# When a second MoE's weight splits begin and when its token lists are read: one planner change

## The chip, the cores and the metric

The kernel runs on one core of one Trainium2 chip. The metric is device time in microseconds, the median of repeated executions. A profiled execution, taken once, gives the trace. The engines are named as in the profile: PE (TensorE matmul), PEld (its weight loads), DVE (VectorE), ACT (ScalarE), POOL (GpSimd) and SP (SyncE, which here only issues transfers and reads values out of memory into registers).

## The reference, cut to what matters

```python
x = attention(q, k, v)             # 4 x 576 tokens, 8 heads of 64, causal window of 128
g = softplus(x @ w_in)             # first MoE: 2304 tokens, 512 -> 2048
x = g @ w_out                      #            2048 -> 512
logits = x @ w_gate                # second MoE: 8 experts, top 2
noisy = logits + softplus(x @ w_noise) * noise
top2_w = softmax of the two largest of noisy
for e in range(8):                 # for the tokens that chose expert e
    out[mask] += top2_w * (relu(x[mask] @ w1[e]) @ w2[e])    # 512 -> 1024 -> 512
```

Everything is float32. The kernel keeps precision by splitting a float32 operand into a high and a low part and adding three products (high times high, low times high, high times low).

## The kernel before, in words

**First MoE.** The 2304 tokens are nine chunks of 256. The hidden width of 2048 is cut into 16 slices, and one slice of one chunk is a step: there are 144 steps (`NT`), each of twelve `h` matmuls (512 to 128) and, three steps later, six `y` matmuls (128 to 512). Two PSUM buffers hold `h`, so the `h` of a step can start only when DVE's `sl` (the last operation that reads `h`) of two steps before is done. When a chunk is through, its gate logits, top 2 and ranks are computed (`lg`, the `r_...` rows, `mcum`), and POOL scatters a record of each token and choice into four copies of a table `rect` in memory.

**Second MoE.** Tokens are worked on in groups, each of one expert. Groups 0 to 3 are "early" pairs (256 tokens each), which are counted out as soon as the first six chunks are routed. Then come 14 late "pairs" mixed with five "singles" (128 tokens) and two optional singles. A pair's weights are eight tiles of 512 KB, and its work is eight items, each of twelve `h` matmuls and six `z` or `y` matmuls. For a group the kernel

1. reads the expert and the start of its list from a small table (SP, a value load; tables `c_Eearlyeo`, `c_Lpairseo`, `c_Lsingleseo`, which DVE works out in one-row operations, line 870),
2. reads its list out of the four copies of `rect` (SP, four `rk<-rect` transfers, `g_rows`, line 1031),
3. merges the four (DVE, two `rc<-rk` reductions, lines 1035 and 1036),
4. gathers the tokens (POOL, `xg<-x1buf,rc`, line 1046),
5. transposes them (PE, `t<-ident,xg`, line 201) and splits them into `xh` (ACT) and `xl` (DVE),
6. adds the scaled results into `out` (POOL, `out<-ys,rc`, line 1251).

**Weights.** Line 1110 loads a tile, into one of four extra buffers (`raw2`, shown as `raw`) or into the 24-slot ring that the first MoE's weights also live in (`rawp`). A split makes `whi` of it (ACT, line 1139) and `wlo` (DVE, line 1137). At most five tiles stand split at a time (`NSPLIT`).

**What sets the order.** Each engine runs its instructions in the order in which they were emitted. That order is decided at build time by a planner (`Order`). Work is entered as chains of steps, `chain((engine, cost, function, key, needs), ...)`, with modelled costs in microseconds. A heap pops the step whose modelled time has come, and `after=` puts a chain's first step that much later. `("tab", 0)` marks the early table as given out, `("tab", 1)` the late one. `pump()` issues weight loads as far as buffers and tables allow, and asks for splits as far as the ring has room. The wait of an instruction for its data is added after that and holds up everything behind it on its engine.

Of the kernel before, what the change touches and what calls it, by code (L numbers as in the profile page):

```python
# [25 lines left out]
class Order:  # L26
# [11 lines left out]
    def chain(self, *steps, after=0.0):  # L38

        heapq.heappush(self.heap, (self.now + after, self.count, steps, 0))  # L40
        self.count += 1
# [71 lines left out]
def moe_chain_kernel(ctx, tc, qk, v, w_in, w_out, w_gate, w_noise, noise, w1, w2, out):  # L113
    nc = tc.nc
    PE, ACT, DVE, POOL, SP = nc.tensor, nc.scalar, nc.vector, nc.gpsimd, nc.sync
# [820 lines left out]
    def early_table(c):  # L936
        tb, cnt = counted(c, "E")
        per = tb.above("per", cnt, TB["jfull"], NJ // 2, OP.is_ge)
        inc = tb.upto("inc", per)
        ex, r = tb.first_of(TB["qe"], "q", NEARLY, inc, per)  # L940
        tb.finish("early", ex, r, None, NEARLY)
        a, b = tb.row("a", [E]), tb.row("b", [E])
        tb.tensor_sub(b, inc, per)
        tb.tensor_scalar(a, inc, float(NEARLY), None, op0=OP.min)
        tb.tensor_scalar(b, b, float(NEARLY), None, op0=OP.min)
        tb.tensor_sub(a, a, b)
        off = TB["off"] = tb.row("off", [E])
        tb.tensor_scalar(off, a, 2.0 * P, None, op0=OP.mult)
        chain(*tb.steps, (None, 0.0, early_lists, ("tab", 0), (("scat", c),)))

    def late_table(c):
        tb, cnt = counted(c, "L")
        off, e8, qp, qs_ = TB["off"], TB["e8"], TB["qp"], TB["qs"]
        tb.tensor_sub(cnt, cnt, off)
        me = tb.above("me", cnt, TB["jm"], NJ, OP.is_gt)
        per = tb.above("per", cnt, TB["jpair"], NJ // 2, OP.is_gt)
        se = tb.row("se", [E])
        tb.scalar_tensor_tensor(se, per, -2.0, me, op0=OP.mult, op1=OP.add)
        pinc = tb.upto("pinc", per)
        sinc = tb.upto("sinc", se)  # L960
        ptot, stot = pinc[:, E - 1:E], sinc[:, E - 1:E]


        ex, r = tb.first_of(qp, "A", NLATE, pinc, per, off)
        lastr = tb.row("lastr", [E])
        tb.scalar_tensor_tensor(lastr, per, 2.0 * P, off, op0=OP.mult, op1=OP.add)
        all8 = tb.row("all8", [1])
        tb.tensor_scalar(all8, stot, float(E), None, op0=OP.is_equal)
        ok = tb.row("ok", [NLATE])
        eq = tb.row("eq", [NLATE])  # L970
        tb.tensor_tensor(eq, qp, ptot.to_broadcast([1, NLATE]), OP.is_equal)
        tb.tensor_tensor(eq, eq, all8.to_broadcast([1, NLATE]), OP.mult)
        tb.tensor_tensor(ok, qp, ptot.to_broadcast([1, NLATE]), OP.is_lt)
        tb.tensor_add(ok, ok, eq)
        tb.finish("pairs", ex, r, ok, NLATE)


        gq = tb.row("gq", [NSING])
        tb.tensor_sub(gq, qs_, stot.to_broadcast([1, NSING]))
        half = tb.row("half", [NSING])  # L980
        tb.tensor_scalar(half, gq, 0.0, None, op0=OP.mult)
        for j in range(1, NSING, 2):
            tb.scalar_tensor_tensor(half, gq, float(j), half, op0=OP.is_equal, op1=OP.add)
        gp = tb.row("gp", [NSING])
        tb.tensor_sub(gp, gq, half)
        tb.tensor_scalar(gp, gp, 0.5, float(NLATE), op0=OP.mult, op1=OP.add)
        exb, rb_ = tb.first_of(gp, "B", NSING, pinc, per, off)
        tb.scalar_tensor_tensor(rb_, half, float(P), rb_, op0=OP.mult, op1=OP.add)
        okb = tb.row("okb", [NSING])
        tb.tensor_tensor(okb, gp, ptot.to_broadcast([1, NSING]), OP.is_lt)  # L990
        cm = tb.row("cm", [NSING, E7])
        tb.tensor_tensor(cm, jb(sinc[:, :E7], NSING, E7), ib(qs_, NSING, E7), OP.is_le)
        exs = tb.total("exs", cm, NSING)
        rs = tb.of_expert("rs", exs, lastr, NSING)
        own = tb.row("own", [NSING])
        tb.tensor_tensor(own, qs_, stot.to_broadcast([1, NSING]), OP.is_lt)
        for x, y in ((exb, exs), (rb_, rs)):
            tb.tensor_sub(y, y, x)
            tb.tensor_mul(y, y, own)
            tb.tensor_add(x, x, y)  # L1000
        tb.tensor_max(okb, okb, own)
        used_ = TB["used"] = tb.row("used", [NSING], I32)
        tb.tensor_copy(used_, okb)
        tb.finish("singles", exb, rb_, okb, NSING)
        chain(*tb.steps, (None, 0.0, None, ("tab", 1), (("scat", c),)), (None, 0.0, pump))


    groups = [(2, "early", i) for i in range(NEARLY)]
# [14 lines left out]
    def g_rows(g):  # L1023

        n, eo, i = groups[g]
        eo = TB[eo]
        r0 = SP.value_load(eo[0:1, 1, i:i + 1], min_val=0, max_val=E * T)
        rc = tl(p2, [P, 2, 2], I32, "rc", 6, ("gdone", g))
        rk = tl(p2, [P, NCOPY, 2, 2], I32, "rk", 6, ("rows", g))
        for k in range(NCOPY):  # L1030
            SP.dma_start(rk[:, k, :n, :], rect[k][bass.ds(r0, n * P), :].rearrange("(a p) z -> p a z", p=P))

        def merge():

            DVE.tensor_reduce(rc[:, :n, 0], rk[:, :, :n, 0].rearrange("p k a -> p a k"), axis=AX.X, op=OP.min)
            DVE.tensor_reduce(f32(rc[:, :n, 1]), f32(rk[:, :, :n, 1]).rearrange("p k a -> p a k"), axis=AX.X, op=OP.add)  # L1036
        chain(("V", 0.4, merge, ("rows", g)), after=15.0 if g < NEARLY else 9.0)
        GR[g] = dict(rc=rc)

    def g_gather(g):  # L1040
# [36 lines left out]
    REG, W2, RAW2 = {}, {}, {}  # L1077
    NSPLIT = 5
    NXTRA = 4
    extra, inring, nsplit = set(), [0], [0]  # L1080

    def ring_left():
        return NRING - live1() - inring[0] - 2 * nsplit[0]

    def w2_load():
        j = wl[0]
        if j >= NW:
            return False
        g, kind, f = WJ[j]
        if g >= sure[0] or ("tab", int(g >= NEARLY)) not in o_.fin:  # L1090
            return False
        more = len(extra) < NXTRA
        if not more and (nback[0] < len(sidx) or ring_left() < 1 + 2 * max(1, NSPLIT - nsplit[0])):
            return False
        wl[0] += 1
        n, eo, i = groups[g]
        if g not in REG:
            REG[g] = SP.value_load(TB[eo][0:1, 0, i:i + 1], min_val=0, max_val=E - 1)
            if g >= NEARLY:
                g_rows(g)  # L1100
            if g < 3 or g - 3 in turned:
                g_start(g)
        if more:
            extra.add(j)
            t = p2.tile([P, 1024], F32, name="raw2", tag="raw2", bufs=NXTRA)
        else:
            inring[0] += 1
            t = wpool.tile([P, 1024], F32, name="rawp", tag="w", bufs=NRING)
        RAW2[j] = t
        SP.dma_start(t, (w2 if kind else w1)[bass.ds(REG[g], 1), f].rearrange("e p n -> p (e n)"))  # L1110
        chain(("DMA", (1 << 19) / 280e3, None), (None, 2.0, None, ("r2" if n == 2 else "w2", j)))
        if n == 1 and wsp[0] == j:
            skip_singles()
        return True
# [11 lines left out]
    def w2_split():  # L1126
        skip_singles()
        j = wsp[0]
        if j >= wl[0] or nsplit[0] >= NSPLIT or nback[0] < len(sidx) or ring_left() < 2:
            return False  # L1130
        wsp[0] += 1
        nsplit[0] += 1
        t = RAW2[j]
        hi, lo = W2[j] = [wpool.tile([P, 1024], F32R, name=x, tag="w", bufs=NRING) for x in ("whi", "wlo")]

        def low():
            DVE.tensor_sub(lo, t, f32(hi))  # L1137
            w2_drop(j)
        chain(("A", ca(1024), lambda: ACT.activation(hi, t, AF.Copy), None, (("r2", j),)),  # L1139
              ("V", cv(1024), low, ("w2", j)))  # L1140
        return True

    def w2_drop(j):
# [2 lines left out]
            extra.remove(j)  # L1146
        else:
            inring[0] -= 1

    def early_lists():  # L1150
        for g in range(NEARLY):
            g_rows(g)

    def pump():
        while w2_load():
# [174 lines left out]
    for t in range(NT + max(L2, len(items) + 2)):  # L1330
# [22 lines left out]
            early_table(NCH - 4)  # L1353
        if t == last_start:
            few_t()
        if t < NT:
            c, fc = jobs[t]
            if c == NCH - 1 and fc == 1:
                x_load(0)
            mm1(c * NF + fc)  # L1360
            if c == 0 and fc == NA + 3:
                part_load(0)
            used(2 * fc, c)
            if NT - 3 < t:
                if t == NT - 2:
                    need(("gl", 0))
                g_transpose(0, t - NT + 2)
                if t == NT - 1:
                    turned.add(0)
                    if 3 in REG:  # L1370
                        g_start(3)
        else:
            phase2(t - NT)
# [77 lines left out]
```

## Time and profile before

| | |
|---|---|
| median of 3 runs | 1157.99 us (1157.8 to 1158.23) |
| time of the profiled execution | 1153.89 us |
| its span | 1151.5 us |
| PE busy | 1073.7 us (93%) |
| DVE busy | 749.4 us (65%) |
| ACT busy | 616.6 us (54%) |
| POOL busy | 507.4 us (44%) |
| mean granted TensorE clock | 0.971 |

The span runs from the first instruction to the last one. The profiled execution's own time is 2.4 us above its span, and 4.1 us below the median of the timed runs, so sums that are made in the trace are applied to the median as differences. Busy shares are means over the whole span. The granted clock is given as a share of full speed: 1.00 is 2.4 GHz and 0.50 is 1.2 GHz.

### The profile page before, as it was taken

The numbers are of one execution on the slowest core, as the hardware profiler recorded it, in microseconds if no ns is written. First come the engines' busy times: TensorE is split into PE (matmuls) and PEld (weight loads), VectorE is DVE, ScalarE is ACT, GpSimd is POOL, SyncE is SP. The second block draws the span as 40 slices with busy tenths as digits, with TensorE's granted clock in tenths as the row PEclk, the third lists the DMA queues.
The fourth block names the chain that finished last, engine by engine and source line by source line (L and its number), as shares of the span: only waits on it lengthen the run. The fifth ranks groups of instructions, "written<-read, shape, count | busy, mean of one in ns | idle before, by whom it ended". The sixth has DMA issues, their size and how long they took to land.

```text
span 1151.5 us, 20919 instructions
## 1 busy us (share of the span) xinstructions
PE 1073.7 (93%) x7021; PEld 915.6 (80%) x7021; DVE 749.4 (65%) x1946; ACT 616.6 (54%) x1459; POOL 507.4 (44%) x535
## 2 busy tenths in 40 slices
PE   5589999999999999999789996899999999999997
PEld 3467777787789888888578885797997997999984
DVE  8975799988775777777477685453553553555520
ACT  7876778877664444444244553354454553555531
POOL 3455667866675666666366131122321321322112
PEclk8799999999999999999989998899999999999999
DMA  7231454554683321222249729588888888888822
GB/s 301 101 92 56 179 186 139 206 201 163 202 297 104 110 73 57 74 75 74 59 145 332 220 30 310 181 217 239 265 222 258 245 222 263 243 225 229 216 61 37
DMA packets 96556, 198.90 MB, mean 173 GB/s; under 512 B 34048, under 2 KB 44800, under 8 KB 96448
## 3 DMA queue, kind: packets, MB, share of 16 engines
q1 hardware_dynamic: 86112, 176.01, 46.8%
q0 software_dynamic: 10336, 21.54, 9.4%
q8 instruction: 56, 0.92, 0.3%
q14 instruction: 52, 0.43, 0.1%
HBM read 157.82 MB, written 39.69 MB: 172 GB/s over the span
## 4 chain that ended last, share of the span: by engine, by line
PE 77%; DVE 11%; DMA 4%; ACT 4%; issue 2%; SPq 1%; POOL 1%; POOLq 0%; ACTq 0%
PE h L190 35%; PE y L190 23%; PE z L190 10%; PE t L201 4%; PE t L190 3%; PE t L339 2%; DMA raw<-in_moe_w_out 1%; DVE s L350 1%; ACT s L356 1%; DVE w L504 1%; DMA out<-ys,rc 1%; DVE cva L495 1%; DVE cva L496 1%; DVE cva L494 1%; DVE gl L572 1%
## 5 line engine op out<-in xcount | busy, mean ns | idle before, releaser
L190 PE MATMUL h<-xh,w 128*128 128x256 f32 x1152 | 239.5, 291 | 9.5 <-DVE sl L568 9.4
L1251 POOL DMA_INDIRECT out<-ys,rc x41 | 81.5, 1987 | 306.0 <-DVE ys L1260 137.1
L190 PEld LDWEIGHTS h<-xh,w 128*128 128x128 f32 x1152 | 191.5, 193 | 23.5 <-DVE sl L568 14.5
L1137 DVE TENSOR_TENSOR wlo<-rawp,whi 128x1024 fp32r<-128x1024 f32 x105 | 128.3, 1222 | 119.4 <-ACT whi L1139 119.3
L190 PE MATMUL y<-w,gh 128*128 128x512 f32 x552 | 180.8, 409 | 0.1
L1139 ACT ACTIVATE whi<-rawp 128x1024 fp32r<-128x1024 f32 x105 | 111.3, 1060 | 119.0 <-PE h L190 88.9
L190 PE MATMUL h<-xl,w 128*128 128x256 f32 x576 | 164.5, 286 | 3.1 <-DVE xl L434 3.1
L574 POOL TENSOR_TENSOR su<-sa,su 128x256 f32<-128x256 f32 x144 | 113.5, 788 | 119.0 <-DVE su L573 105.5
L190 PE MATMUL h<-xh,whi 128*128 128x256 f32 x576 | 164.8, 286 | 0.0
L190 PE MATMUL h<-xl,whi 128*128 128x256 f32 x576 | 162.8, 283 | 0.0
L190 PE MATMUL h<-xh,wlo 128*128 128x256 f32 x576 | 162.8, 283 | 0.0
L565 ACT ACTIVATE sa<-h 128x256 f32<-128x256 f32 x144 | 55.0, 382 | 157.9 <-PE h L190 130.4
L569 POOL TENSOR_TENSOR sl<-sl,su 128x256 f32<-128x256 f32 x144 | 111.3, 774 | 17.1 <-DVE sl L568 5.7
L190 PEld LDWEIGHTS h<-xl,w 128*128 128x128 f32 x576 | 111.5, 194 | 6.6 <-DVE xl L434 3.5
L190 PEld LDWEIGHTS h<-xh,whi 128*128 128x128 f32 x576 | 109.6, 190 | 7.2 <-DVE rc L1036 0.7
L190 PEld LDWEIGHTS h<-xl,whi 128*128 128x128 f32 x576 | 109.7, 190 | 7.1 <-issue 1.4
L190 PEld LDWEIGHTS h<-xh,wlo 128*128 128x128 f32 x576 | 109.7, 190 | 0.0
L190 PE MATMUL y<-w,gl 128*128 128x512 f32 x276 | 109.5, 397 | 0.0
L190 PEld LDWEIGHTS y<-w,gh 128*128 128x128 f32 x552 | 95.9, 193 | 17.0 <-issue 2.9
L370 POOL TENSOR_TENSOR s<-s,st 128x512 f32<-128x512 f32 (+2 forms) x72 | 72.4, 1013 | 33.1 <-DVE st L362 19.0
L573 DVE TENSOR_SCALAR su<-sa 128x256 f32<-128x256 f32 x144 | 61.7, 428 | 38.6 <-ACT sa L566 37.9
L572 DVE TENSOR_TENSOR gl<-sl,gh 128x256 fp32r<-128x256 f32 x144 | 80.7, 561 | 9.3 <-ACT gh L570 6.6
(258 smaller groups left out, 2265.8 us busy)
## 6 DMA issues: line engine op xcount, KB each, us to landing
rawp<-in_moe_w SPq DMA_DIRECT2D x135, 512.0 KB, 4.6
raw<-in_moe_w SPq DMA_DIRECT2D x49, 512.0 KB, 4.4
qkT<-in_qk SPq DMA_DIRECT2D x20, 512.0 KB, 5.2
raw<-in_moe_w_in SPq DMA_DIRECT2D x16, 512.0 KB, 5.2
raw<-in_moe_w_out SPq DMA_DIRECT2D x16, 512.0 KB, 6.5
out<-zero SPq DMA_DIRECT2D x19, 256.0 KB, 5.4
xspill<-xh SPq DMA_DIRECT2D x9, 512.0 KB, 2.6
xspill<-xl SPq DMA_DIRECT2D x9, 512.0 KB, 3.9
```

The lines of the kernel that those rows point to most:

```text
L190: PE.matmul(o, l, r, start=start, stop=stop)
L201: PE.transpose(o, i, idn)
L339: PE.matmul(ps[j][:nq, x, :n].rearrange("p (s t) -> p s t", t=P), qkT[hd, u % NQK, 0, hp, :nq], qkT[hd, sl, 1, hp, :], start=True, stop=True)
L370: POOL.tensor_tensor(s[:nq, :, :n], s[:nq, :, :n], st[:nq, 3, 2 * x:2 * x + 2, None].to_broadcast([nq, 2, n]), OP.mult)
L565: chain(("A", ca(CT), lambda: ACT.activation(a, ph, AF.Abs)), ("A", ca(CT), lambda: ACT.activation(a, a, AF.Exp, scale=-1.0), ("e", t)), ( ...
L569: ("P", cg(CT), lambda: POOL.tensor_add(l, l, u), None, (("d", t),)),
L572: ("V", cv(CT), lambda: DVE.tensor_sub(gl, l, f32(gh)), ("g", t)))
L573: chain(("V", cv2(CT), lambda: DVE.tensor_scalar(u, a, 1.0, 1.0, op0=OP.add, op1=OP.subtract), None, (("e", t),)), ("P", cg(CT), lambda: P ...
L574: ("P", cg(CT), lambda: POOL.tensor_tensor(u, a, u, OP.subtract), ("d", t)), after=2 * ca(CT) + 0.15)
L1137: DVE.tensor_sub(lo, t, f32(hi))
L1139: chain(("A", ca(1024), lambda: ACT.activation(hi, t, AF.Copy), None, (("r2", j),)), ("V", cv(1024), low, ("w2", j)))
L1251: POOL.indirect_dma_start(out=out[:, :], out_offset=bass.IndirectOffsetOnAxis(ap=rc[:, a, 0:1], axis=0), in_=ys, in_offset=None, compute_o ...
```

## The change

Four things change in the planner's calls.

- `early_lists`, which issued the list reads of all four early groups (16 transfers) when the early table was ready, is gone. Now `w2_load` calls `g_rows` for every group when the first weight tile of that group is loaded.
- The late table is given out in two parts. After the pairs part, `("tab", 1)` is set and `pump` is called. After the singles part, `("tab", 2)` is set and `pump` is called again. A single's load asks for `("tab", 2)`.
- The merge of a list is planned 8.8 us after its reads (6.0 plus 0.7 for each of four copies), where it was 15.0 for the early groups and 9.0 for the others. SP is now modelled as busy 2.8 us for the four reads and 0.5 us for a weight load, whose landing is modelled 0.5 us longer.
- `w2_split` does nothing until the step `NT - 4`, and at that step `pump` is called.

```diff
@@ early_table
-        chain(*tb.steps, (None, 0.0, early_lists, ("tab", 0), (("scat", c),)))
+        chain(*tb.steps, (None, 0.0, None, ("tab", 0), (("scat", c),)), (None, 0.0, pump))
@@ late_table
         tb.finish("pairs", ex, r, ok, NLATE)
+        tb.steps += [(None, 0.0, None, ("tab", 1), (("scat", c),)), (None, 0.0, pump)]
...
         tb.finish("singles", exb, rb_, okb, NSING)
-        chain(*tb.steps, (None, 0.0, None, ("tab", 1), (("scat", c),)), (None, 0.0, pump))
+        chain(*tb.steps, (None, 0.0, None, ("tab", 2)), (None, 0.0, pump))
@@ g_rows
-        chain(("V", 0.4, merge, ("rows", g)), after=15.0 if g < NEARLY else 9.0)
+        chain(("SP", 0.7 * NCOPY, None))
+        chain(("V", 0.4, merge, ("rows", g)), after=6.0 + 0.7 * NCOPY)
@@ w2_load
-        if g >= sure[0] or ("tab", int(g >= NEARLY)) not in o_.fin:
+        if g >= sure[0] or ("tab", 2 if groups[g][0] == 1 else int(g >= NEARLY)) not in o_.fin:
...
-            if g >= NEARLY:
-                g_rows(g)
+            g_rows(g)
...
-        chain(("DMA", (1 << 19) / 280e3, None), (None, 2.0, None, ("r2" if n == 2 else "w2", j)))
+        chain(("SP", 0.5, None), ("DMA", (1 << 19) / 280e3, None), (None, 2.5, None, ("r2" if n == 2 else "w2", j)))
@@ w2_split
-        if j >= wl[0] or nsplit[0] >= NSPLIT or nback[0] < len(sidx) or ring_left() < 2:
+        if j >= wl[0] or not splitting[0] or nsplit[0] >= NSPLIT or nback[0] < len(sidx) or ring_left() < 2:
@@ main loop
+        if t == NT - 4:
+            splitting[0] = True
+            pump()
```

PE's order stays. What moves on the other engines is shown at three places. Line numbers of the changed kernel are one to two off those of before.

**First place: DVE, some twenty steps before the first MoE's end, just after the early table.** `wlo` is the DVE half of a weight split, `su`, `sl`, `gh` and `gl` are a step's own operations, and `lg` and `r_u` belong to the routing of a chunk. Before:

```order
L572 TENSOR_TENSOR gl<-sl,gh 128x256
L573 TENSOR_SCALAR su<-sa 128x256
L568 SCALAR_TENSOR_TENSOR sl<-h,sl 128x256
L571 CAST gh<-sl 128x256
L572 TENSOR_TENSOR gl<-sl,gh 128x256
L1137 TENSOR_TENSOR wlo<-raw_7510,whi 128x1024
L573 TENSOR_SCALAR su<-sa 128x256
L568 SCALAR_TENSOR_TENSOR sl<-h,sl 128x256
L681 TENSOR_REDUCE lg<-t 128x32
L1137 TENSOR_TENSOR wlo<-raw_7512,whi 128x1024
L573 TENSOR_SCALAR su<-sa 128x256
L704 TENSOR_SCALAR r_u<-r_a 128x16
```

After the change, at the same place:

```order
L571 CAST gh<-sl 128x256
L572 TENSOR_TENSOR gl<-sl,gh 128x256
L573 TENSOR_SCALAR su<-sa 128x256
L568 SCALAR_TENSOR_TENSOR sl<-h,sl 128x256
L571 CAST gh<-sl 128x256
L681 TENSOR_REDUCE lg<-t 128x32
L572 TENSOR_TENSOR gl<-sl,gh 128x256
L573 TENSOR_SCALAR su<-sa 128x256
L704 TENSOR_SCALAR r_u<-r_a 128x16
```

Two weight splits that stood ahead of a step's `su` and `sl` are gone from here.

**Second place: DVE near the end of the first MoE, four steps before its end.** Before:

```order
L572 TENSOR_TENSOR gl<-sl,gh 128x256
L573 TENSOR_SCALAR su<-sa 128x256
L571 CAST gh<-sl 128x256
L568 SCALAR_TENSOR_TENSOR sl<-h,sl 128x256
L572 TENSOR_TENSOR gl<-sl,gh 128x256
L681 TENSOR_REDUCE lg<-t 128x32
L571 CAST gh<-sl 128x256
L573 TENSOR_SCALAR su<-sa 128x256
L572 TENSOR_TENSOR gl<-sl,gh 128x256
L704 TENSOR_SCALAR r_u<-r_a 128x16
L568 SCALAR_TENSOR_TENSOR sl<-h,sl 128x256
```

After the change:

```order
L568 SCALAR_TENSOR_TENSOR sl<-h,sl 128x256
L571 CAST gh<-sl 128x256
L572 TENSOR_TENSOR gl<-sl,gh 128x256
L1139 TENSOR_TENSOR wlo<-raw_7456,whi 128x1024
L1139 TENSOR_TENSOR wlo<-raw_7458,whi 128x1024
L1139 TENSOR_TENSOR wlo<-raw_7460,whi 128x1024
L681 TENSOR_REDUCE lg<-t 128x32
L1139 TENSOR_TENSOR wlo<-raw_7462,whi 128x1024
L1139 TENSOR_TENSOR wlo<-rawp,whi 128x1024
L573 TENSOR_SCALAR su<-sa 128x256 x2
L704 TENSOR_SCALAR r_u<-r_a 128x16
L568 SCALAR_TENSOR_TENSOR sl<-h,sl 128x256 x2
```

Five splits now stand together ahead of a step's `su` and `sl`. ACT has its five `whi` in a row at the same step.

**Third place: DVE at the end of the third early group (group 2), where the late table is worked out.** The `c_L...` rows are the singles part of the table, `xl` and `gl` are operations of items, and `rc<-rk` are merges of lists. Before, the first merges after the early groups' ones, for groups 4 and 5, stand behind the whole table:

```order
L870 TENSOR_SCALAR c_LBr<-c_LBr 1x7
L1190 SCALAR_TENSOR_TENSOR gl<-h,gh 128x256
L870 CAST c_Lsingleseo<-c_LBr 1x7
L870 CAST c_Lsingleseo<-c_LBex 1x7
L1035 TENSOR_REDUCE rc<-rk 128x2
L1036 TENSOR_REDUCE rc<-rk 128x2
L1035 TENSOR_REDUCE rc<-rk 128x2
L1036 TENSOR_REDUCE rc<-rk 128x2
```

After the change, the merges of group 4 and of group 5 stand here:

```order
L1067 TENSOR_TENSOR xl<-t,xh 128x4x128
L1036 TENSOR_REDUCE rc<-rk 128x2
L1037 TENSOR_REDUCE rc<-rk 128x2
L870 TENSOR_TENSOR c_LBofoh<-c_LBex,c_e_7160 1x56
L1139 TENSOR_TENSOR wlo<-raw_8450,whi 128x1024
L1188 SCALAR_TENSOR_TENSOR gl<-h,gh 128x256
L870 TENSOR_TENSOR c_LBofoh<-c_LBofoh,c_Eoff 1x56
L1036 TENSOR_REDUCE rc<-rk 128x2
L1037 TENSOR_REDUCE rc<-rk 128x2
L870 TENSOR_REDUCE c_LBof<-c_LBofoh 1x7
L870 TENSOR_TENSOR c_LBr<-c_LBr,c_LBof 1x7
L870 SCALAR_TENSOR_TENSOR c_LBr<-c_Lhalf,c_LBr 1x7
```

Both merges moved ahead of the remainder of the singles part and of the splits and `gl` of the next items. On POOL the four gathers of groups 4 and 5 correspondingly moved ahead of the two `out<-ys` of group 2. On SP eight weight loads stand between the list reads of group 4 and those of group 5, as before.

## Rows read from the trace of the kernel before

**Rows 1.** Waits of PE, 540 to 1152 us: total, times, longest

```profile
PE t L201 <- DMA xg<-x1buf,rc: 14.6, 1, 14.6
PE h L190 <- DVE sl L568: 8.4, 1, 8.4
PE t L190 <- DVE mcum L757: 3.5, 2, 2.0
PE t L190 <- DVE r_mb L704: 3.2, 1, 3.2
```

**Rows 2.** By window: busy us of five engines, PEclk, DMA share, GB/s

```profile
573.20:583.40 10.20, 5.59 (x20) 5.02 (x21) 6.96 (x17) 5.29 (x13) 5.21 (x6) 0.50 0.89 341
593.60:597.10 3.50, 3.50 (x13) 2.92 (x12) 1.86 (x9) 2.05 (x4) 1.98 (x2) 0.51 0.01 0
713.10:726.80 13.70, 2.86 (x9) 2.51 (x10) 0.69 (x1) 0.60 (x1) 5.44 (x5) 0.50 0.88 318
```

**Rows 3.** Timeline of SP, 556 to 612 us: start, length

```profile
559.21 11.32 SPq L1031 DMA_DIRECT2D rk<-rect  x16
571.34 1.94 SPq L1110 DMA_DIRECT2D raw<-in_moe_w  x4
```

**Rows 4.** Timeline of DVE, 560 to 592 us

```profile
575.99 1.23 DVE L1137 TENSOR_TENSOR wlo<-raw,whi 128x1024 fp32r<-128x1024 f32 x1 [11.31 <-ACT whi L1139]
```

**Rows 5.** The page's groups, the two halves of a split: busy, mean ns

```profile
L1137 DVE TENSOR_TENSOR wlo<-rawp,whi 128x1024 fp32r<-128x1024 f32 x105 | 128.3, 1222 | 119.4 <-ACT whi L1139 119.3
...
L1139 ACT ACTIVATE whi<-rawp 128x1024 fp32r<-128x1024 f32 x105 | 111.3, 1060 | 119.0 <-PE h L190 88.9
```

**Rows 6.** Timeline of DVE, 612 to 622 us

```profile
613.15 0.42 DVE L568 SCALAR_TENSOR_TENSOR sl<-h,sl 128x256 f32<-128x256 f32 x1
```

**Rows 7.** Timeline of PE: first matmul of one h, two places

```profile
615.98 0.28 PE L190 MATMUL h<-xh,w 128*128 128x256 f32 x1
...
702.08 0.28 PE L190 MATMUL h<-xh,whi 128*128 128x256 f32 x1
```

**Rows 8.** Waits of SP's sequencer, 555 to 720 us

```profile
SPq L1098 <- DVE c_Lpairseo L870: 24.9, 1, 24.9
```

**Rows 9.** Timeline of SP, 655 to 720 us

```profile
686.02 3.24 SPq L1031 DMA_DIRECT2D rk<-rect  x4
...
702.38 2.34 SPq L1031 DMA_DIRECT2D rk<-rect  x4
704.95 5.88 SPq L1110 DMA_DIRECT2D rawp<-in_moe_w  x8
```

**Rows 10.** Timeline of DVE, 680 to 725 us

```profile
693.07 0.69 DVE L1065 TENSOR_TENSOR xl<-t,xh 128x512 fp32r<-128x512 f32 x1 [0.23 <-ACT xh L1064]
...
696.01 0.20 DVE L870 TENSOR_TENSOR c_LBofoh<-c_LBofoh,c_Eoff 1x56 f32<-1x56 f32 x1
...
698.49 0.42 DVE L1190 SCALAR_TENSOR_TENSOR gl<-h,gh 128x256 fp32r<-128x256 f32 x1 [0.23 <-ACT gh L1189]
...
710.25 0.14 DVE L1035 TENSOR_REDUCE rc<-rk 128x2 int32<-128x8 int32 x1
```

**Rows 11.** Timeline of POOL, 684 to 726 us

```profile
687.96 1.57 POOL L1251 DMA_INDIRECT out<-ys,rc  x1 [3.88 <-DVE c_Lgp L870]
...
715.34 1.55 POOL L1251 DMA_INDIRECT out<-ys,rc  x1 [7.90 <-DMA out<-ys,rc]
717.20 1.01 POOL L1046 DMA_INDIRECT xg<-x1buf,rc  x1 [0.30 <-issue]
```

**Rows 12.** Landing, tile view: rk 559:572, rk 712:717, rawp 704.9:712, xg 716:722

```profile
DMA to landing us min/median/max: 1.8/1.8/2.2
...
DMA to landing us min/median/max: 5.8/7.5/8.2
...
DMA to landing us min/median/max: 5.3/7.5/10.0
...
DMA to landing us min/median/max: 4.7/4.7/4.7
```

More of the change, by code (lines that the diff above doesn't have):

```diff
@@ L1079, in moe_chain_kernel @@
     NXTRA = 4
+    splitting = [False]
     extra, inring, nsplit = set(), [0], [0]
@@ L1148, in w2_drop @@
             inring[0] -= 1
-    def early_lists():
-        for g in range(NEARLY):
-            g_rows(g)
     def pump():
```

## The prediction

> **What bounds the kernel now.** I looked first at what PE waits for, because its busy share of 93% leaves little else to gain. From 540 us on, PE waits five times in all [rows 1]: 14.6 us once for gathered tokens, 8.4 us once for a step's `sl`, 3.2 us once for a routing mask (`r_mb`), and 3.5 us in two waits for the running count `mcum`. After the 14.6 us wait, which ends at 723.9 us, the list shows nothing more, so the 428 us behind it are matmul time that this change does not touch. Next comes the granted clock by windows [rows 2]. It is at half, 1.2 GHz, in three stretches (a fourth is the last 5 us of the kernel, after its matmuls have thinned out). Two begin in a long wait and outlast it, and the second begins 1.4 us after the `r_mb` wait has ended. The `mcum` waits, at most 2.0 us long, are followed by no such stretch. In the three stretches PE worked 5.59, 3.50 and 2.86 us at half clock, so they cost half of that: 2.8, 1.7 and 1.4 us. The two big waits and the middle one therefore hold 8.4 + 2.8 + 3.2 + 1.7 + 14.6 + 1.4 = 32.1 us.
>
> Then I asked what stands in front of each wait on the engine that ends it.
>
> The 8.4 us: SP issues all 16 list reads of the early groups in 11.3 us, and only then the four first weight tiles, from 571.34 us on [rows 3]. DVE sits idle 11.31 us, because the next instruction in its order is a weight split that needs such a tile, and behind that split stand `su` and `sl` of the step that PE waits for [rows 4].
>
> The 14.6 us: SP waits 24.9 us for the pairs table [rows 8] and reads the list of group 4 at 686.02 us [rows 9]. The merges of groups 4 and 5 do not run before 710.25 us, at the end of the singles table [rows 10]. By then POOL stands in an `out<-ys` of group 2 which waits another 7.90 us for a scatter, so the first gather starts at 717.20 us [rows 11] and lands 4.7 us later [rows 12].
>
> **The change part by part.** *No split before step NT - 4.* At the early table, no `wlo` stands on DVE ahead of the step any more (first place of the orders). The 8.4 us and its 2.8 us of half clock go. Nothing new waits there: the list of group 0 is read in the same place as now, and lands in 1.8 to 2.2 us [rows 12].
>
> The 3.2 us wait for `r_mb` comes from a routing chain that was pushed back by the same splits. Of the four chunks routed in this stretch, the other three made PE wait 3.5 us together, 1.2 us each. So I take 1.2 us as what stays, and 2.0 us as gained, with the 1.7 us of clock.
>
> *The splits come in one lump.* At step NT - 4 five `wlo` stand on DVE ahead of a step's `sl` (second place). One takes 1.22 us [rows 5], the five 6.1 us. Before, this `sl` ended at 613.57 us [rows 6] and PE needed it at 615.98 us [rows 7], 2.4 us of cover. That leaves 3.7 us, and with the small operations that now also stand ahead of it (another `su`, a routing row) I take 4.0 us of waiting on PE. It is less, 2.5 us, if DVE starts the lump 1.5 us earlier than it reaches that `sl` now. It is more, 5.4 us, if the `gl` that stood behind the `sl` ahead of it must wait first. ACT's five `whi` at 1.06 us run one ahead of the `wlo` and add no more. The shortest wait that half clock followed is 3.2 us, so I add one such stretch, 1.7 us.
>
> *Lists group by group and the late table in two parts.* SP still waits for the pairs table, which is not worked out any earlier, and reads group 4's list as now. What changes is that the merge of group 4 stands right behind the `xl` that ends at 693.76 us [rows 10], and by then its list has long landed: the reads are issued by 689.3 us [rows 9] and took about 2 us more. POOL is free, since its first `out` of this stretch ends at 689.53 us [rows 11] and the two of group 2, which it waited in, now come behind the gathers. Two gathers of 1.0 us and 4.7 us to land put the tokens there at about 701 us. PE needs them at 723.9 - 14.6 = 709.3 us. So the 14.6 us and 1.4 us go, with 8 us to spare.
>
> *A new wait on DVE.* The merge of group 5 now stands right behind a table row that ends at 696.21 us [rows 10], ahead of the split and the `gl` of the next item. Its list stands on SP behind eight loads. Eight such loads take 5.88 us to issue and four list reads 2.34 us [rows 9], so from 689.5 us on the lists are issued by 697.8 us. Their landing is bounded by 2.2 us (idle queue) and 8.2 us (behind eight loads) [rows 12]: 700.0 to 706.0 us. I take 703.5 us. The nearest row is that of a burst of eight loads: from the first one's landing at 704.95 + 5.3 = 710.2 us to the last one's at 710.5 + 10.0 = 720.5 us they land 1.47 us apart. Here the first would land at about 693.5 us and the last about 703.8 us, and the lists are behind them. DVE then stands 7.3 us. The `gl` behind the merge ended 2.7 us after that table row [rows 10], so it ends at about 706.2 us, and PE needs it at 702.08 us [rows 7]: 4.1 us of waiting, 0.6 to 6.6 by the bounds, and again 1.7 us of clock.
>
> The Trainium skill bears on this wait from two sides ("DMA: Bandwidth & Descriptors"). Its section "Anatomy of one DMA — SWDGE (gpsimd) path" gives a transfer a fixed cost of about 2.0 us, which agrees with the 1.8 us of the idle list reads, though those are SP's. By that alone the list would land at 699.8 us, 0.4 us would be given back here instead of 5.8, and the sum would be 1133.2 us. "Queues, rings and completion order" says that each DMA engine consumes the descriptors of a queue row in ring order, which would put a list behind the loads issued ahead of it; the 7.5 us row agrees with this one.
>
> *Merges of groups 1 to 3.* Each of their lists is now read behind loads too, some of which wait for a `wlo` of the lump. By the order, each merge stands behind rows that themselves come after these loads, with about 2 to 4 us to spare by my estimate. I cost them at nothing; if that cover is gone, each costs PE what the list is late, and rival C is that case.
>
> *The modelled SP times, and the rest.* They only move where the planner puts things. The number of instructions on each engine is nearly the same, and nothing becomes cheaper.
>
> **Sum.** Gained: 8.4 + 2.8 + 2.0 + 1.7 + 14.6 + 1.4 = 30.9 us. Given back: 4.0 + 1.7 + 4.1 + 1.7 = 11.5 us. Net 19.4 us. The profiled execution would go from 1153.89 to 1134.5 us. The median lies 4.1 us above it, and I apply the difference there: 1157.99 - 19.4 = **1138.6 us**. With the bounds of the two new waits (3.1 us without clock, to 15.4 us) and 1 us either way for `r_mb`, this case spans 1129 to 1144 us.
>
> **Rivals.** *A*, the forecast, 0.50.
>
> *B: both new waits are covered.* The lump starts early enough, or the list lands soon. Time 1157.99 - 30.9 = 1127.1 us. For it: DVE has slack without the early splits. Against it: five splits are 6.1 us and the cover is 2.4 us. 0.14.
>
> *C: more merges wait than that of group 5.* Two of the merges of groups 1 to 3 stop DVE too, 3 us of PE each with 1.7 us of clock: 1138.6 + 9.4 = 1148.0 us. For it: those lists also stand behind loads, and the merge is planned 8.8 us behind its reads, where a list of group 6 took up to 8.2 us and its turn on SP comes on top. Against it: the margins named above. The Trainium skill's "Rules for kernel authors" on the same page advises to issue a transfer early and wait on it late, which an earlier merge goes against; the rows bear it out as far as group 5. 0.14.
>
> *D: the late stall stays.* The pairs table still comes at about 684 us; if group 4's gather were held by something else, 16.0 us would stay, and the 5.8 us at group 5 would not be paid: 1138.6 + 16.0 - 5.8 = 1148.8 us. Against it: on POOL nothing but finished work stands ahead of those gathers. 0.09.
>
> *E: slower.* SP, DVE and PE form a chain: the list of group 2 stands on SP behind loads that wait for buffers which the splits and PE give back, and the merge that waits for it holds up those very splits and the `gl` that PE needs. If this held DVE as long as SP now waits for a table, 24.9 us [rows 8], the time would be 1138.6 + 24.9 = 1163.5 us. It decides the sign once the wait is over 19.4 us. Against it: every load ahead of that list waits for a split or a matmul that comes before the merge in its own engine's order, so the wait ends with the lump. 0.08.
>
> The remaining 0.05 is for small losses that add up to about no change.
>
> **How the numbers follow.** The time is A's. The range, 1127 to 1149 us, holds A, nearly all of B to D, and leaves out E, the rest, and a little on either side, under 0.2. 0.2% or 2.3 us is about what a measurement of this kernel can tell from no change. Faster by more than that: A to D, 0.87. Within it: 0.05. Slower: E, 0.08.
>
> **What would show it.** PE's list of waits should lose the 8.4 us `sl` at the early table and the 14.6 us for `xg`. It should have a wait of about 4 us for an `sl` near the end of the first MoE, behind five `wlo` in a row, and one of about 4 us for a `gl` some 7 us after DVE stopped at a merge whose releaser is an `rk` transfer. The clock should show half-speed stretches after these two only. I am wrong if DVE stops at a merge of groups 1 to 3, if the `xg` wait is still there, or if PE shows neither new wait.

## The result and the profile after

The changed kernel takes 1136.95 us (median of 4 runs, 1136.42 to 1141.57), the kernel before 1157.89 us in the runs beside it. The ratio is 0.9829, with a 95% interval of 0.9803 to 0.9855: 21 us less, where 19.4 were forecast. The profiled execution takes 1136.42 us with a span of 1134.2 us, 17.3 us less than the span before; the timed runs of before lie 3 to 4 us above its profiled execution, while that of after is the lowest of its runs and 0.5 us below their median.

PE's list of waits after the change, over the same part of the program (line, releaser, total us, times, longest), answers to [rows 1]:

```profile
PE h L190 <- DVE gl L1188: 6.5, 1, 6.5
PE t L190 <- DVE mcum L757: 3.5, 2, 2.0
PE h L190 <- DVE sl L568: 3.3, 1, 3.3
PE t L190 <- DVE r_mb L704: 0.6, 1, 0.6
```

The waits for `xg` and for `sl` at the early table are gone, and the two waits for `mcum` are what they were. The 0.6 us for `r_mb` are not a remainder of the 3.2 us. That wait was at the chunk that is routed just after the early table, and there PE now takes `r_mb` without waiting. The 0.6 us are at the next chunk, behind the new lump of splits, where PE did not wait before. On PE's timeline the two chunks before the change:

```profile
592.22 0.18 PE L190 MATMUL t<-r_mb,tri 128*128 128x8 bf16 x1 [3.18 <-DVE r_mb L704]
...
625.48 0.18 PE L190 MATMUL t<-r_mb,tri 128*128 128x8 bf16 x1
```

and after it:

```profile
577.94 0.18 PE L190 MATMUL t<-r_mb,tri 128*128 128x8 bf16 x1
...
615.50 0.18 PE L190 MATMUL t<-r_mb,tri 128*128 128x8 bf16 x1 [0.60 <-DVE r_mb L704]
```

Two new waits stand in the list, of an `sl` and of a `gl`, at the two places that the forecast named. The granted clock is at half after each of them (busy us of PE, PEld, DVE, ACT, POOL, then PEclk, DMA share, GB/s; compare [rows 2]):

```profile
603.90:607.30 3.40, 3.40 (x17) 3.40 (x17) 2.62 (x11) 0.46 (x2) 2.14 (x3) 0.50 0.81 318
696.00:702.80 6.80, 4.05 (x16) 3.76 (x17) 5.02 (x19) 1.30 (x2) 3.02 (x2) 0.50 1.00 377
```

PE worked 3.40 and 4.05 us in these two stretches, so they cost 1.7 and 2.0 us.

The first new wait on DVE's timeline (start, length, idle time before and its releaser in brackets):

```profile
596.26 3.49 DVE L1139 TENSOR_TENSOR wlo<-raw,whi 128x1024 fp32r<-128x1024 f32 x3
599.66 0.25 DVE L681 TENSOR_REDUCE lg<-t 128x32 f32<-128x96 f32 x1
599.83 1.21 DVE L1139 TENSOR_TENSOR wlo<-raw,whi 128x1024 fp32r<-128x1024 f32 x1
600.96 1.22 DVE L1139 TENSOR_TENSOR wlo<-rawp,whi 128x1024 fp32r<-128x1024 f32 x1
602.10 0.49 DVE L573 TENSOR_SCALAR su<-sa 128x256 f32<-128x256 f32 x2
...
603.14 0.74 DVE L568 SCALAR_TENSOR_TENSOR sl<-h,sl 128x256 f32<-128x256 f32 x2
```

Five `wlo` run from 596.26 to 602.18 us with only a routing row between them, and the `sl` that PE waits for ends behind them. PE stood from 600.34 to 603.60 us.

The second new wait begins on SP. Eight loads lie between the list reads of group 4 and those of group 5:

```profile
676.01 3.07 SPq L1032 DMA_DIRECT2D rk<-rect  x4
679.41 4.71 SPq L1112 DMA_DIRECT2D rawp<-in_moe_w  x8
685.48 3.48 SPq L1032 DMA_DIRECT2D rk<-rect  x4
```

On DVE the merge of group 4 does not wait, and that of group 5 waits 9.23 us, with a split and the `gl` of the next item behind it:

```profile
685.25 0.14 DVE L1036 TENSOR_REDUCE rc<-rk 128x2 int32<-128x8 int32 x1
...
686.99 0.20 DVE L870 TENSOR_TENSOR c_LBofoh<-c_LBofoh,c_Eoff 1x56 f32<-1x56 f32 x1
696.42 0.17 DVE L1036 TENSOR_REDUCE rc<-rk 128x2 int32<-128x8 int32 x1 [9.23 <-DMA rk<-rect]
...
697.07 1.22 DVE L1139 TENSOR_TENSOR wlo<-raw,whi 128x1024 fp32r<-128x1024 f32 x1
...
698.29 0.40 DVE L1188 SCALAR_TENSOR_TENSOR gl<-h,gh 128x256 fp32r<-128x256 f32 x1
```

PE needed that `gl` at 692.26 us and got it at 698.69. On POOL the gathers now start at 686 and 697 us and the `out<-ys` of group 2 comes behind them, where before the gathers stood behind it [rows 11]:

```profile
686.18 1.43 POOL L1048 DMA_INDIRECT xg<-x1buf,rc  x1 [6.52 <-PE h L190]
...
697.33 1.79 POOL L1048 DMA_INDIRECT xg<-x1buf,rc  x1 [8.41 <-issue]
...
705.61 1.90 POOL L1249 DMA_INDIRECT out<-ys,rc  x1 [4.96 <-ACT gh L1187]
```

### The profile page after: what moved, and what is told of

The parts are those of the page before. It is cut to its first block, busy times and chain, and to the rows that moved or that the text cites. A ratio compares the mean times of both kernels' runs of the same rounds, so it can differ in the third digit from the quotient of the medians.

```text
span 1134.2 us, 20933 instructions
## 1 busy us (share of the span) xinstructions
PE 1071.8 (94%) x7021; PEld 914.2 (81%) x7021; DVE 748.8 (66%) x1946; ACT 616.2 (54%) x1459; POOL 509.9 (45%) x535
## 4 chain that ended last, share of the span: by engine, by line
PE 76%; DVE 11%; DMA 5%; ACT 3%; issue 2%; POOL 1%; SPq 1%; POOLq 0%; DVEq 0%; ACTq 0%
PE h L190 35%; PE y L190 24%; PE z L190 10%; PE t L201 4%; PE t L190 3%; PE t L339 2%; DMA raw<-in_moe_w_out 1%; DVE s L350 1%; ACT s L356 1%; DVE w L504 1%; DVE cva L495 1%; DMA rawp<-in_moe_w 1%; DVE cva L496 1%; DVE cva L494 1%; DVE su L573 1%
## 5 line engine op out<-in xcount | busy, mean ns | idle before, releaser
L1139 DVE TENSOR_TENSOR wlo<-rawp,whi 128x1024 fp32r<-128x1024 f32 x107 | 130.7, 1222 | 133.8 <-ACT whi L1141 127.4
L569 POOL TENSOR_TENSOR sl<-sl,su 128x256 f32<-128x256 f32 x144 | 109.7, 762 | 17.3 <-DVE sl L568 5.8
L1048 POOL DMA_INDIRECT xg<-x1buf,rc x41 | 42.4, 1035 | 105.6 <-DVE rc L1037 60.4
L370 POOL TENSOR_TENSOR s<-s,st 128x512 f32<-128x512 f32 (+2 forms) x72 | 72.2, 1011 | 33.2 <-DVE st L362 19.4
```

The lines of the kernel that those rows point to most:

```text
L370: POOL.tensor_tensor(s[:nq, :, :n], s[:nq, :, :n], st[:nq, 3, 2 * x:2 * x + 2, None].to_broadcast([nq, 2, n]), OP.mult)
L569: ("P", cg(CT), lambda: POOL.tensor_add(l, l, u), None, (("d", t),)),
L1048: POOL.indirect_dma_start(out=x, out_offset=None, in_=x1buf[:T - 3 * CT if g < NEARLY else TPAD, :], in_offset=bass.IndirectOffsetOnAxis(a ...
```

## The experiments

Times are medians. Each kernel was timed against the kernel before on the same chip (1156.2 to 1157.9 us there), and the ratio and its 95% interval are to that.

| kernel | us | ratio | interval |
|---|---|---|---|
| the change | 1136.95 | 0.9829 | 0.9803 to 0.9855 |
| x1, splits from the early table on | 1136.74 | 0.9834 | 0.9817 to 0.9850 |
| x2, the 16 list reads at once | 1140.78 | 0.9862 | 0.9846 to 0.9879 |
| x3, late table in one piece | 1143.10 | 0.9887 | 0.9871 to 0.9904 |
| x4, planned times of before | 1129.80 | 0.9773 | 0.9753 to 0.9792 |
| x5, next list ahead | 1129.93 | 0.9779 | 0.9765 to 0.9792 |
| x6, splits spread from the twelfth step | 1137.99 | 0.9851 | 0.9834 to 0.9867 |
| x7, x5 and x6 | 1128.55 | 0.9765 | 0.9750 to 0.9781 |
| x8, x5 and splits spread from the eighth step | 1124.91 | 0.9718 | 0.9701 to 0.9734 |
| x9, late merges planned 7 us later | 1131.01 | 0.9780 | 0.9756 to 0.9805 |
| x10, before with the split rule alone | 1142.01 | 0.9873 | 0.9856 to 0.9890 |

**x10: one part alone.** Of the change, only the rule on splits is put into the kernel before.

```diff
-        if j >= wl[0] or nsplit[0] >= NSPLIT or nback[0] < len(sidx) or ring_left() < 2:
+        if j >= wl[0] or not splitting[0] or nsplit[0] >= NSPLIT or nback[0] < len(sidx) or ring_left() < 2:
...
+        if t == NT - 4:
+            splitting[0] = True
+            pump()
```

> The kernel of before with one part of the change alone: no split before the fourth step from the end. Theory (the early wait came from a split in DVE's order, and the rest is independent of it): the 8.4 us wait and its 2.8 us are gone, the r_mb wait shrinks from 3.2 to 0.6 us without its half clock (4.3 us), the lump costs 5.0 us, the wait of 14.6 us for tokens stays: 1156.5 - 10.5 = about 1146 us. Rival (the 16 list reads have a share in the early wait): a wait of over 2 us stays at the early table, 1149 us or more.

Measured: 1142.01 us. PE's waits no longer hold one for `sl` at the early table, although the 16 list reads, on SP from 559.40 to 570.46 us, are still in front of the first tile. At the `r_mb` of the chunk that is routed there PE stands 0.6 us instead of 3.2. So without the split in DVE's order both waits go, and the rival falls. The wait for tokens is not the 14.6 us that I expected to stay, but 10.7, and the time is 4 us below the 1146 us of the theory:

```profile
PE t L201 <- DMA xg<-x1buf,rc: 10.7, 1, 10.7
...
PE h L190 <- DVE sl L568: 3.0, 1, 3.0
```

On POOL (start, length, idle before) the second `out<-ys` of group 2 waits 4.23 us for the first to land, where it waited 7.90 us before [rows 11]:

```profile
695.81 1.55 POOL L1252 DMA_INDIRECT out<-ys,rc  x1 [15.29 <-ACT ys L1258]
701.59 1.55 POOL L1252 DMA_INDIRECT out<-ys,rc  x1 [4.23 <-DMA out<-ys,rc]
703.44 1.01 POOL L1046 DMA_INDIRECT xg<-x1buf,rc  x1 [0.30 <-issue]
```

In the kernel before, the first of the two started at 705.9 us, just after the eight loads began at 704.95 us [rows 9]; here it starts at 695.8 us, and the eight loads begin at 703.6 us. So some 4 us of the late wait went with the splits. That the scatter was slowed by the loads is my reading; no run varied that alone.

**x3: the late table in one piece.**

```diff
-        tb.steps += [(None, 0.0, None, ("tab", 1), (("scat", c),)), (None, 0.0, pump)]
...
-        chain(*tb.steps, (None, 0.0, None, ("tab", 2)), (None, 0.0, pump))
+        chain(*tb.steps, (None, 0.0, None, ("tab", 1), (("scat", c),)), (None, 0.0, None, ("tab", 2)), (None, 0.0, pump))
```

> The changed kernel with the late table given out in one piece again. Theory (the merges of groups 4 and 5 came late because the planner only learned of the pairs at the end of the singles part): both merges stand behind the singles table again, the wait for gathered tokens of about 14 us and its 1.4 us of clock are back, the wait of 6.5 us at the merge of group 5 with its 2.0 us of clock is gone: 1137 + 16 - 8.5 = about 1144.5 us. Rival (the earlier planned merge, 8.8 us behind the reads, is what moved them): the merges stay where they are in the changed kernel, and the time is 1137 us.

Measured: 1143.10 us. Both merges are behind the singles table again, and PE waits for tokens, 10.9 us where x10 has 10.7 and the theory had about 14:

```profile
PE t L201 <- DMA xg<-x1buf,rc: 10.9, 1, 10.9
```

The planned 8.8 us alone do not move the merges; the rival falls. Giving out the pairs first is worth the 6.2 us between this kernel and the change. x3 holds everything but this part, x10 only the split rule, and they are within 1.1 us of each other. So the split rule and the late table make the gain. The other two parts, the lists group by group and the planned times, add nothing that shows in sum while the late table is in one piece; x2 and x4 take them out of the change one at a time.

**x1: splits from the early table on, lists still group by group.**

```diff
-    splitting = [False]
+    splitting = [True]
...
-        if t == NT - 4:
-            splitting[0] = True
-            pump()
```

> The changed kernel with its splits allowed from the early table on again, as before; the lists stay group by group. Theory (the 8.4 us wait came from the first weight tiles, which stood on SP behind 16 list reads, with a split of them in DVE's order ahead of a step): four list reads take about 3 us of SP where 16 took 11.3, so the first tile comes some 8 us earlier and the wait is gone or under 2 us. The lump of five splits is gone too (3.3 us of wait and 1.7 us of clock in the changed kernel): about 1132 us. Rival (any split ahead of a step's sl at that place stops PE): the 8.4 us wait and its half clock, 11 us, are back, less 5 us for the lump: about 1143 us.

Measured: 1136.74 us, against 1132 by the theory. The 8.4 us wait does not come back, and the lump's `sl` wait is gone, as the theory had it. The 8.4 us therefore took two things together: a split ahead of the step in DVE's order, which x10 took away, and its tile late behind 16 list reads, which is away here. What the theory missed is the wait for `r_mb`, 3.7 us at the chunk where the change has none, with a half-clock stretch:

```profile
PE t L190 <- DVE r_mb L704: 3.7, 1, 3.7
```

On DVE the splits stand between the rows of the routing chain that ends in `r_mb`:

```profile
570.99 0.71 DVE L704 TENSOR_TENSOR r_u<-r_a,r_u 128x16 f32<-128x16 f32 x1
571.62 1.21 DVE L1139 TENSOR_TENSOR wlo<-raw,whi 128x1024 fp32r<-128x1024 f32 x1
...
573.09 0.16 DVE L704 SCALAR_TENSOR_TENSOR r_l<-lg,r_l 128x16 f32<-128x16 f32 x1
573.18 1.21 DVE L1139 TENSOR_TENSOR wlo<-raw,whi 128x1024 fp32r<-128x1024 f32 x1
574.31 0.16 DVE L704 TENSOR_TENSOR r_l<-r_l,r_u 128x16 f32<-128x16 f32 x1
```

**x2: the 16 list reads at once again.** `early_lists` is called when the early table is ready, and `w2_load` reads only the late groups' lists.

```diff
-        chain(*tb.steps, (None, 0.0, None, ("tab", 0), (("scat", c),)), (None, 0.0, pump))
+        chain(*tb.steps, (None, 0.0, early_lists, ("tab", 0), (("scat", c),)), (None, 0.0, pump))
...
-            g_rows(g)
+            if g >= NEARLY:
+                g_rows(g)
```

> The changed kernel with the 16 list reads of the early groups issued together again; splits still begin four steps before the end. Theory (DVE's order counts, and no split stands there any more): SP is busy 11 us again and the first weight tile comes late, but nobody waits for it: within 2 us of the changed kernel's 1137 us, with no wait on sl at the early table. Rival (the 16 reads themselves hold up something a step needs, or the reads group by group behind loads cost the changed kernel something that this gives back): a wait of several us at the early table, 1143 us or more, or a gain of over 2 us.

Measured: 1140.78 us, 3.8 us over the change, so neither number held. No `sl` wait is at the early table, as the theory said. But all four merges, still planned 8.8 us behind their reads, stand early on DVE, and one waits for its list:

```profile
DVE rc L1036 <- DMA rk<-rect: 3.4, 1, 3.4
```

That falls into the same routing chain, and PE waits for `r_mb` (the lump's `sl` wait is still there, 2.7 us):

```profile
PE t L190 <- DVE r_mb L704: 3.7, 1, 3.7
```

So with merges planned this early, reading the lists group by group is worth 3.8 us. In x10 the merges of these groups are planned 15 us behind the 16 reads, and none of this shows.

**x5: the next group's list ahead of the loads.**

```diff
-            g_rows(g)
+            for g1 in (g, g + 1):
+                if g1 not in GR and g1 < sure[0] and ("tab", 2 if groups[g1][0] == 1 else int(g1 >= NEARLY)) in o_.fin:
+                    g_rows(g1)
```

> The changed kernel, with the list of the next group read together with a group's own, ahead of that group's eight weight loads (if the table with it is there). Theory (the 6.5 us wait of PE comes from DVE standing at the merge of group 5, whose list lay behind eight loads): the list of group 5 lands about 2 us after its reads, DVE does not stop, and the 6.5 us and 2.0 us of half clock are gone: about 1128.5 us. Rival (DVE would stop or PE would wait there anyway, for the weight tiles, which now come some 4 us later, or for the next list): 1133 us or more.

Measured: 1129.93 us, 1.4 us above the theory and 3 us below the rival, and its profiled span is 1125.6 us, 8.6 us under that of the change. SP reads two lists, four copies each, and then loads:

```profile
676.07 6.06 SPq L1032 DMA_DIRECT2D rk<-rect  x8
682.37 7.83 SPq L1114 DMA_DIRECT2D rawp<-in_moe_w  x11
```

DVE does not stop at a merge any more, and PE has no `gl` wait:

```profile
PE h L190 <- DVE sl L568: 2.9, 1, 2.9
PE t L190 <- DVE r_mb L704: 0.6, 2, 0.4
```

The cause of the second new wait is shown: the list behind eight loads, and the merge ahead of the `gl`.

**x9: the merge later, the reads where they are.**

```diff
-        chain(("V", 0.4, merge, ("rows", g)), after=6.0 + 0.7 * NCOPY)
+        chain(("V", 0.4, merge, ("rows", g)), after=6.0 + 0.7 * NCOPY + (7.0 if g >= NEARLY else 0.0))
```

> The changed kernel with the merges of the late groups planned 7 us later, nothing else; in DVE's order the merges of groups 4 and 5 then stand together behind two more splits and the gl of two more items. Theory (the list of group 5 is not late for its gather, only the merge stands too early in DVE's order): DVE still stops, for 5 us or less, and PE waits under 1.5 us; the gathers still come before PE needs them; 1128.5 to 1131 us. Rival (the gathers of groups 4 and 5 need the early merge): PE waits for gathered tokens again, 1137 us or more.

Measured: 1131.01 us (five of six runs from 1129.0 to 1131.2 us, one at 1138.4). DVE stops 2.2 us at a merge and PE has no `gl` wait; the gathers come only 0.8 us late:

```profile
PE h L190 <- DVE sl L568: 3.3, 1, 3.3
PE t L201 <- DMA xg<-x1buf,rc: 0.8, 1, 0.8
```

So the list was early enough for its tokens to within 0.8 us, and it was the merge's place on DVE that cost time.

**x4: the planned times of before.** The merges are planned 15.0 and 9.0 us behind the reads, and SP's modelled costs are taken out, with the 0.5 us of landing.

```diff
-        chain(("SP", 0.7 * NCOPY, None))
-        chain(("V", 0.4, merge, ("rows", g)), after=6.0 + 0.7 * NCOPY)
+        chain(("V", 0.4, merge, ("rows", g)), after=15.0 if g < NEARLY else 9.0)
...
-        chain(("SP", 0.5, None), ("DMA", (1 << 19) / 280e3, None), (None, 2.5, None, ("r2" if n == 2 else "w2", j)))
+        chain(("DMA", (1 << 19) / 280e3, None), (None, 2.0, None, ("r2" if n == 2 else "w2", j)))
```

> The changed kernel with the planned merge times (15.0 and 9.0 us) and the modelled SP and landing costs of before. Theory (these only shift places by a few rows): the merges of groups 4 and 5 stand nearly where they do in the changed kernel, and DVE still stops at that of group 5: 1135 to 1139 us. Rival (the planned 8.8 us are too short, and set the wait of 6.5 us): with 9.0 and the merge a few rows later the wait shrinks by more than 3 us, and the time is below 1134 us.

Measured: 1129.80 us, 7 us under the change. My theory fell here, and the rival's number held: these planned times set the second wait. DVE waits 3.07 us at the merge of group 5, which now comes behind one more split and one more `gl`:

```profile
688.59 0.41 DVE L1187 SCALAR_TENSOR_TENSOR gl<-h,gh 128x256 fp32r<-128x256 f32 x1
...
692.14 0.17 DVE L1036 TENSOR_REDUCE rc<-rk 128x2 int32<-128x8 int32 x1 [3.07 <-DMA rk<-rect]
```

The `gl` wait of PE is down to 0.2 us:

```profile
PE t L190 <- DVE mcum L757: 4.5, 2, 3.0
PE h L190 <- DVE sl L568: 3.1, 1, 3.1
PE h L190 <- DVE gl L1187: 0.2, 1, 0.2
```

Two things moved together. The merge stands later, and SP reads group 5's list from 681.0 us on instead of 685.5, since the pairs table is given out one split earlier. x9 shows that the first is enough.

**x6, x7 and x8: the lump taken apart.** `splitting` becomes a number of tiles that may stand split. In x6 it grows by one at every second step from the twelfth before the end on; x7 is x5 and x6 together; in x8, with x5, it grows at every step from the eighth on.

```diff
-        if j >= wl[0] or not splitting[0] or nsplit[0] >= NSPLIT or nback[0] < len(sidx) or ring_left() < 2:
+        if j >= wl[0] or nsplit[0] >= splitting[0] or nback[0] < len(sidx) or ring_left() < 2:
...
-        if t == NT - 4:
-            splitting[0] = True
+        if NT - 8 <= t and splitting[0] < NSPLIT:
+            splitting[0] += 1
             pump()
```

> The changed kernel, with the splits let in one at a time: one more at every second step from the twelfth before the end on, instead of five at the fourth. Theory (the 3.3 us wait for sl comes from five splits in a row on DVE, and one of 1.2 us fits in a step's slack): that wait and its 1.7 us of half clock are gone: about 1132 us. Rival (DVE has no slack near the end of the first MoE, and single splits delay other steps as much in sum): 1136 us or more.

> Both of the two edits before it, the list of the next group ahead and the splits one at a time. Theory (the two waits are independent): both gains add, 13.5 us, about 1123.5 us. Rival (with one wait gone another takes its place): less than 9 us of gain, 1128 us or more.

> The next group's list ahead, and the splits let in one at a time again, but one at every step from the eighth before the end on, so that the first comes behind the routing chain of the chunk that made PE wait 3.6 us for r_mb when the spread began at the twelfth. Theory (a single split fits in a step's slack, and the r_mb wait was a split inside that routing chain): neither the sl wait of 2.9 us nor the r_mb wait, and no half clock before the end: 4.5 us under the kernel with the next list ahead alone, about 1125.5 us. Rival (DVE and ACT have no slack anywhere in the last steps): a wait of 2 us or more in another place, 1128 us or more.

Measured: x6 1137.99 us, no gain over the change, as its rival had it. The `sl` wait is gone, but the first split, from 572.48 us on, fell into the routing chain, and an `r_mb` wait took its place:

```profile
PE h L190 <- DVE gl L1188: 6.5, 1, 6.5
PE t L190 <- DVE r_mb L704: 3.8, 1, 3.8
```

x7 has the same `r_mb` wait, 3.6 us, and its 1128.55 us does not show a gain over x5; here too the rival's number held. In x8 the chain ends in `r_mb` at 580.35 us and the first split starts at 584.59 us. It takes 1124.91 us, the fastest of all, 12 us under the change; its interval does not meet that of x5. PE's waits there:

```profile
PE t L190 <- DVE mcum L757: 3.5, 2, 2.0
PE h L190 <- DVE sl L568: 0.7, 1, 0.7
PE t L190 <- DVE r_mb L704: 0.4, 1, 0.4
```

So a single split has room in a step behind that chain, and in these runs it had none inside the chain. The forecast of 1125.5 us for x8 held in the time. Its theory did not hold whole: a half-clock stretch, worth 1.7 us, follows a wait for `mcum` in the profiled execution, which is the slowest of its five runs (last section).

## Why the prediction was right

Point by point, with the forecast's terms:

- *The 8.4 us and 2.8 us at the early table:* gone, and x10 shows that the split rule alone does it; in x1 the lists group by group do it too.
- *`r_mb`, 2.0 us and 1.7 us of clock:* 2.6 and 1.7 in sum, but not as I had it. I let 1.2 us stay, from the 3.5 us for `mcum`, which I read as waits of the other chunks. They are not: PE stands for `mcum` at the counts for the two tables, at 549.55 and 662.61 us in the trace before, and at the `r_mb` of the other chunks it did not stand at all. At its own chunk the whole 3.2 us went, and 0.6 us came up at the next one; x10 has the lump without it, so its cause stays open. That the same splits made this wait is shown by x10, where 0.6 us of it is left, and by x1 and x6, where splits in the chain bring it back.
- *The late wait, 14.6 us and 1.4 us:* gone. The cause was only partly the one I gave: x3 and x10 show that about 11 us of it hung on the place of the merges, and the other 4 us went with the splits already.
- *The lump, 4.0 us and 1.7 us:* 3.3 and 1.7.
- *The merge of group 5, 4.1 us and 1.7 us:* 6.5 and 2.0. The mechanism held (x5, x9), and the mis-sized term is mainly the landing of the list. I took it from the pitch at which a burst of eight loads lands, 5.7 us behind the end of the reads' issue. It landed 7.5 us behind it (688.96 to 696.42 us), which is the median of the reads behind eight loads [rows 12], and DVE stood 9.2 us instead of 7.3. The `gl` was done 11.5 us behind the table row where I had 10.0, and PE needed it 5.1 us behind that row where I had 5.9.
- *Merges of groups 1 to 3 at nothing:* DVE waits for a list at one merge only, that of group 5.

Summed from the trace: gained 8.4 + 2.8 + 2.6 + 1.7 + 14.6 + 1.4 = 31.5 us, given back 3.3 + 1.7 + 6.5 + 2.0 = 13.5 us, 18.0 us net, where the two spans differ by 17.3 us. The forecast's 19.4 us was 1.4 us too much by this sum: the `gl` wait cost 2.7 us more than forecast, and the lump and `r_mb` 1.3 us less. The medians moved 3.5 us more than the profiled executions, because the profiled execution of before lies 4 us below the median of its runs and that of after only 0.5 us. That the median came out within 1.7 us of the forecast is therefore partly luck; the trace bears out the parts to within these errors.

Of the rivals, B (both new waits covered) is refuted by the two new waits, and x8 shows that what B describes can nearly be had by other edits: 1124.9 us against the 1127.1 us worked out for it. C, D and E did not occur. What C feared, a merge of an early group that stops DVE, occurs in other kernels: in x2 for 3.4 us, behind the 16 reads and not behind loads, and in x8 for 1.3 us, without a wait of PE.

Left open: whether the list of group 5 is late because its transfers stand behind the loads in SP's queue, or because the loads keep the transfer engines busy. x5 removes both. The Trainium skill ("DMA: Bandwidth & Descriptors", "Queues, rings and completion order") says that on each DMA engine descriptors are consumed in ring order. That agrees with the first, but no run here tells the two apart. The same page ("Anatomy of one DMA — SWDGE (gpsimd) path") gives a transfer that GpSimd issues a fixed cost of about 2.0 us. These reads, which SP issues, show more behind a burst: issued from 685.48 to 688.96 us, they ended DVE's wait at 696.42 us.

## What to carry to other kernels

On an engine that runs in order, a wait costs what stands behind it, not what waits for it: a split or a merge that nobody needs yet cost PE 3 to 8 us here, because a small operation of the current step stood behind it. So work that is free to move is best placed singly, behind the last operation of a chain that has no slack, and a wait on a transfer is best placed late, or its transfer ahead of the bulk loads. When a stall is removed, the parts of a change should be tried one at a time: here two of four made the gain, a third, the planned times, cost 7 us beside the rest, and the fourth, the lists group by group, was worth 3.8 us beside that third and was not tried without it.

## What the runs showed of the hardware that was not expected

The length of a PE wait does not by itself say whether the clock drops after it. In x4 a wait of 3.04 us for `mcum` was followed by full clock (this window begins 0.17 us behind its end):

```profile
655.00:660.00 5.00, 5.00 (x33) 4.49 (x33) 4.58 (x18) 1.33 (x2) 2.76 (x1) 1.00 0.02 5
```

In x8 a wait of 1.97 us at the same place in the program was followed by 3.5 us at half:

```profile
650.10:653.60 3.50, 3.41 (x11) 2.83 (x12) 2.78 (x9) 1.06 (x1) 1.16 (x1) 0.51 0.24 43
```

Waits of 1.97 us at that place in the kernels before and after were not. The lump's `sl` wait shows the same: 2.72 us in x2 were followed by full clock, 2.89 us in x5 by half. My price for a new wait, one half-clock stretch each, rested on the waits of one trace and is no rule; what decides it was not tried.
